# A 2:4-pruned matrix product on one core: six packed tiles and nine pruning pieces in place of seven and six

## The chip, the cores and the metric

The kernel runs on one core of one Trainium2 chip. The metric is device time of one execution in microseconds, lower is better. The time before is the median of seven runs, 235.54 us (235.22 to 235.74).

The engines that matter are TensorE (PE, matrix products and transposes), VectorE (DVE, elementwise), ScalarE (ACT, elementwise copies and absolute values, and an issuer of DMAs) and SyncE (SP, an issuer of DMAs). Each runs its own instructions in order and waits on semaphores for the others.

## The reference

`x` is 16 x 512 x 1024, `w` is 1024 x 1024, `b` has 1024 elements, all bf16. Within each group of four consecutive rows of `w`, and for each column, the entries whose magnitude is at least the second largest of the four are kept, the others become zero. Then x times the pruned w, plus b:

```python
    wg = w.reshape(G, M, D)                       # M = 4, N = 2
    mag = jnp.abs(wg)
    order = jnp.argsort(mag, 1)
    thr = jnp.take_along_axis(mag, order[:, M - N:M - N + 1, :], 1)
    mask = (lambda x, dt: x.astype(dt))(mag >= thr, w.dtype)
    wp = (wg * mask).reshape(D, D)
    return jnp.einsum("bsd,df->bsf", x, wp) + b
```

## The kernel before

The 8192 rows of x are 64 tiles of 128 rows. A tile needs x transposed (the contraction over 1024 runs along partitions, in 8 steps) and the pruned weights in two halves of 512 columns, `FH`.

**Two ways for a tile.** While the weights are being pruned, they lie in a packed layout: partition q holds the four rows of group q, for each of two halves g of the groups (`w_sb`, `wp`; 512 of the 1024 rows each). The first `NPK` = 7 tiles are multiplied straight from that layout, by columns as soon as these are pruned ("packed tiles"). Their x is loaded plainly by `load_x` (line 97), transposed on PE (`transpose`, line 188, tokens `T6a`: tile 6, half g = 0) and copied from PSUM by ACT (`copy_xt`, line 197, tokens `C6a`). The product of tile t with pruning piece i is `mm_piece` (line 208, tokens `M6.1`): four matmuls, one for each row of the group, of as many columns as the piece has. Meanwhile `save` (line 179) writes the pruned weights to a scratch tensor in DRAM and `reload` (line 182) reads them back in natural order into `wp_nat`, one half of the columns at a time. The other 57 tiles ("natural tiles") take x by transposing DMA (`load_batch`, line 239), in batches of 5, 4 and then 8 tiles with three buffers, and 16 matmuls of 512 columns each. Batch 0 is done one column half at a time (line 370), all others a tile at a time (line 380). DVE adds the bias on the way from PSUM (`evac`, line 362).

**Pruning.** `Piece` (line 140) prunes a block of columns of one g in eight steps: absolute value (`abs`), pairwise maximum and minimum (`hi`, `lo`), minimum and maximum of these (`t1`, `t2`), the threshold (`thr`), the comparison (`mask`) and the product (`mult`). Six pieces stand in line 123: four of 256 columns, then two of 512. For the first two, `abs` runs on DVE (line 161), for the others on ACT (line 154). Piece 0 does `mask` and `mult` in two parts, x and y, of two rows of the group each.

**What sets the order.** Lines 251 to 267 write out the order of each engine's work by hand, as lists of tokens; `run` (line 331) emits them as dependences allow, and `seq` (line 61) pins each engine to it. Tokens `F5` are fillers: products of zeros (line 129) that keep PE occupied. Ahead of the list stand 6 fillers of 512 columns and 8 of 128 (lines 341 and 342). After the list: four saves on SP, the first transposed batch, the two reloads, two more batches, and `finish` (line 231) for the packed tiles: their first column half was set aside by ACT (`stage`, line 226, tokens `S5`), the second is still in PSUM; DVE adds the bias to both and ACT issues the store. Two saves (tokens `W5`, `W4`) are issued by ACT.

**Queues.** Loads are issued in the order of lines 104 to 120, all by SP except x tile 6's first half, which ACT issues ahead of its table load (line 106). Every DMA takes one of eight semaphores in turn, and is not issued before the one eight places ahead of it, from either queue, has landed. PSUM has six buffers for products (`psum_o`), one tile's half in each, and two for transposes.

Of the kernel before, what the change touches and what calls it, by code (L numbers as in the profile page):

```python
# [10 lines left out]
def kernel(  # L11
# [8 lines left out]
    P = 128  # L20
    bf16 = mybir.dt.bfloat16
    fp32 = mybir.dt.float32
# [5 lines left out]
    Dout = w.shape[1]  # L28
# [3 lines left out]
    NT = NTOK // P  # L32
    FH = 512
# [3 lines left out]
    xf = x.flatten_outer_dims()  # L37
    of = out.flatten_outer_dims()

    NPK = 7  # L40
    batches = []
    t0 = NPK
    while t0 < NT:
        nb = min((5, 4)[len(batches)] if len(batches) < 2 else 8, NT - t0)
        batches.append((t0, nb))
        t0 += nb

    const = ctx.enter_context(tc.tile_pool(name="const", bufs=1))
    dram = ctx.enter_context(tc.tile_pool(name="dram", bufs=1, space=bass.MemoryType.DRAM))
# [44 lines left out]
    def load_w(g, c0, c1, eng="sp"):  # L94
        issue(eng, w_sb[:, g, :, c0:c1], wv[:, g, :, c0:c1])

    def load_x(ta, tb, g, eng="sp"):
        xs = const.tile([P, tb - ta, HK], bf16, name=f"x_{ta}_{g}")
        issue(eng, xs[:], xv[:, ta:tb, g * HK:(g + 1) * HK])
        for t in range(ta, tb):  # L100
            x_sb[(t, g)] = xs[:, t - ta, :]


    load_w(0, 0, 256)
    load_x(6, 7, 0, "act")
    act(nc.scalar.activation(spark[:, :1], zeros[:, :1], Act.Abs))
    load_x(4, 6, 0)
    load_x(2, 4, 0)
    load_w(0, 256, 512)
    load_x(6, 7, 1)  # L110
    load_x(1, 2, 0)
    load_w(1, 256, 512)
    load_x(2, 4, 1)
    load_w(1, 0, 256)
    load_x(4, 6, 1)
    load_w(0, 512, 1024)
    load_x(0, 2, 1)
    load_x(0, 1, 0)
    load_w(1, 512, 1024)
    sp(nc.sync.dma_start(bias_sb[:], b.partition_broadcast(P)))  # L120


    pieces = [(0, 0, 256), (0, 256, 512), (1, 0, 256), (1, 256, 512), (0, 512, 1024), (1, 512, 1024)]

    ident = const.tile([P, P], bf16)
    make_identity(nc, ident[:])
# [52 lines left out]
    def save(g, c0, c1, eng="sp"):  # L179
        issue(eng, scr_pk[:, g, :, c0:c1], wp[:, g, :, c0:c1])  # L180

    def reload(h):
        fs = slice(h * FH, (h + 1) * FH)
        sp(nc.sync.dma_start(wp_nat[:, :, fs], scr_nat[:, :, fs]))
# [52 lines left out]
    xnat = {}  # L237

    def load_batch(bi):
        if bi >= len(batches):  # L240
            return
        tb, nb = batches[bi]
        xb = xtb.tile([P, KT, 8 * P], bf16, name="xb")
        sp(nc.sync.dma_start_transpose(out=xb[:, :, :nb * P], in_=xf[tb * P:(tb + nb) * P, :]))
        for j in range(nb):
            xnat[tb + j] = xb[:, :, j * P:(j + 1) * P]
# [3 lines left out]

    order = {
        "pe": (
            "T6a F5 T5a T4a F6 T3a T2a F7 M5.0y M4.0y M6.0y M2.0y M5.0x M3.0x T6b T1a M6.0x M3.0y "
            "M4.0x M2.0x M1.0y M1.0x T3b T2b M6.1 M4.1 M3.1 T4b M1.1 M5.1 T5b M2.1 M6.3 M3.3 M4.3 "
            "T1b T0b M5.3 M2.3 M1.3 M3.2 M6.2 M5.2 T0a M4.2 M2.2 M1.2 M0.0y M0.1 M0.2 M0.3 M0.0x "
            "M2.4 M3.4 M1.4 M0.4 M5.4 M4.4 M5.5 M2.5 M1.5 M4.5 M6.4 M0.5 M6.5 M3.5"
        ),
        "dve": (
            "abs0 hi0 lo0 t10 t20 thr0 mask0y mask0x mult0y abs1 mult0x hi1 lo1 t11 t21 thr1 mask1 "
            "mult1 lo3 hi3 t23 t13 thr3 mask3 mult3 lo2 hi2 t22 t12 thr2 mask2 mult2 lo4 hi4 t24 "  # L260
            "t14 thr4 mask4 mult4 hi5 lo5 t25 t15 thr5 mask5 mult5"
        ),
        "act": (
            "C6a C5a C4a C2a C3a C6b C1a abs3 C3b abs2 C2b C4b C5b abs4 C1b abs5 C0a S5 C0b S1 S4 "
            "S6 S2 S0 S3 W5 W4"
        ),
    }
    written = set()
# [4 lines left out]
    def all_of(tok, i):  # L273
        return [tok + x for x in halves.get(i, ("",))]
# [3 lines left out]
        return (tok[:-1] if k else tok), k  # L278

    transposed = []  # L280

    def needs(eng, tok):
        base, k = split_tok(tok)
        if tok[0] == "C":
            return ["T" + tok[1:]]
        if tok[0] == "T":
            return ["C" + transposed[-2]] if len(transposed) > 1 else []
        if tok[0] == "F":
            return []
        if base[0] == "M":  # L290
            t, i = base[1:].split(".")
            key = (int(t), pieces[int(i)][1] // FH)
            slot = []
            if key not in opened and len(opened) >= 6:
                pt, ph = opened[len(opened) - 6]
                slot = [f"S{pt}"] if ph == 0 else []
            return [f"C{t}{'ab'[pieces[int(i)][0]]}", f"mult{i}{k}"] + slot
        if tok[0] == "S":
            return [f"M{tok[1:]}.{n}" for i, pc in enumerate(pieces) if pc[1] < FH for n in all_of(str(i), i)]
        if tok[0] == "W":  # L300
            return all_of("mult" + tok[1:], int(tok[1:]))
        i, step = base[-1], base[:-1]
        before = {"abs": [], "hi": ["abs"], "lo": ["abs"], "t1": ["hi"], "t2": ["lo"],
                  "thr": ["t1", "t2"], "mask": ["thr", "hi", "lo"], "mult": ["mask"]}[step]
        return [b_ + i + (k if b_ == "mask" else "") for b_ in before]

    def emit(eng, tok):
        base, k = split_tok(tok)
        if tok[0] == "T":
            transpose(int(tok[1]), "ab".index(tok[2]))  # L310
            transposed.append(tok[1:])
        elif tok[0] == "F":
            filler(int(tok[1:]))
        elif tok[0] == "C":
            copy_xt(int(tok[1]), "ab".index(tok[2]))
        elif tok[0] == "M":
            mm_piece(*map(int, base[1:].split(".")), part[k])
        elif tok[0] == "S":
            stage(int(tok[1:]))
        elif tok[0] == "W":  # L320
            save(*pieces[int(tok[1:])], eng="act")
        else:
            i = int(base[-1])
            if i not in p:
                p[i] = Piece(i)
            if eng == "act":
                p[i].abs_act()
            else:
                p[i].do(base[:-1], part[k])
# [17 lines left out]
    save(1, 256, 512)  # L347
    load_batch(0)
    reload(0)
    reload(1)  # L350
    load_batch(1)
    load_batch(2)
    for t in (2, 0, 3, 1, 6, 5, 4):
        finish(t)


    def nat_group(xt, ps, c0, c1):
        for kt in range(KT):
            pe(nc.tensor.matmul(ps, lhsT=xt[:, kt, :], rhs=wp_nat[:, kt, c0:c1],  # L359
                                start=(kt == 0), stop=(kt == KT - 1)))  # L360

    def evac(o, ps, c0, c1):
        dve(nc.vector.tensor_tensor(o[:, c0:c1], ps, bias_sb[:, c0:c1], op=Alu.add))  # L363

    def store(eng, t, o, c0=0, c1=Dout):
        issue(eng, of[t * P:(t + 1) * P, c0:c1], o[:, c0:c1])

    for bi, (tb, nb) in enumerate(batches):
        load_batch(bi + 3)
        if bi == 0:  # L370
            outs = [outp.tile([P, Dout], bf16, name="o") for _ in range(nb)]
            for h in range(2):
                for j in range(nb):
                    ps = psum_o.tile([P, FH], fp32, name="ps")
                    nat_group(xnat[tb + j], ps[:], h * FH, (h + 1) * FH)
                    evac(outs[j], ps[:], h * FH, (h + 1) * FH)
                    if h == 1:
                        store("act", tb + j, outs[j])
            continue
        for j in range(nb):  # L380
            t = tb + j
            xt = xnat[t]
            o = outp.tile([P, Dout], bf16, name="o")
            if t == NT - 1:
                for n, (c0, c1) in enumerate(((0, FH), (FH, FH + CW), (FH + CW, Dout - P), (Dout - P, Dout))):
                    ps = psum_o.tile([P, FH], fp32, name="ps")
                    nat_group(xt, ps[:, :c1 - c0], c0, c1)
                    evac(o, ps[:, :c1 - c0], c0, c1)
                    store("act" if n % 2 else "sp", t, o, c0, c1)
            else:  # L390
                pss = [psum_o.tile([P, FH], fp32, name="ps") for _ in range(2)]
                for kt in range(KT):
                    for h in range(2):
                        pe(nc.tensor.matmul(pss[h][:], lhsT=xt[:, kt, :],  # L394
                                            rhs=wp_nat[:, kt, h * FH:(h + 1) * FH],
                                            start=(kt == 0), stop=(kt == KT - 1)))
                for h in range(2):
                    evac(o, pss[h][:], h * FH, (h + 1) * FH)
                    if t >= NT - 6:
                        store("act", t, o, h * FH, (h + 1) * FH)  # L400
                if t < NT - 6:
                    store("act", t, o)
# [30 lines left out]
```

## Time and profile before

| what | us |
|---|---|
| median of seven runs | 235.54 |
| the profiled execution's own time | 235.31 |
| its span, first to last instruction | 233.5 |
| PE busy, natural products of whole tiles (line 394) | 176.3 |
| PE busy, packed products (line 219) | 25.5 |
| PE busy, products done by column half, batch 0 and the last tile (line 359) | 21.1 |
| PE busy, fillers (line 131) | 5.5 |
| PE busy, transposes (line 194) | 5.3 |
| DVE busy in all | 104.3 |
| ACT busy in all | 15.4 |

The span runs from the first to the last instruction of the program; the time of the run also has what lies around it. PE's busy time is modelled at the ends of its matmuls, and what overlaps counts once, so the sums are to be read as shares. The slices of the page (40 of 5.8 us each) show where the engines work: DVE and ACT are dense in the first five slices, the pruning phase, and DVE is at a third or so afterwards.

```profile
PE   8999999999999999999999999999999999999995
DVE  3999559632343343244244234334334424423434
ACT  3678000000000000000000000000000000000000
PEclk9999999999999999999999999999999999999999
DMA  6999979999999972992229921698221221222122
```

### The profile page before, as it was taken

The numbers are of one execution on the slowest core, as the hardware profiler recorded it, in microseconds if no ns is written. First come the engines' busy times: TensorE is split into PE (matmuls) and PEld (weight loads), VectorE is DVE, ScalarE is ACT, GpSimd is POOL, SyncE is SP. The second block draws the span as 40 slices with busy tenths as digits, with TensorE's granted clock in tenths as the row PEclk, the third lists the DMA queues.
The fourth block names the chain that finished last, engine by engine and source line by source line (L and its number), as shares of the span: only waits on it lengthen the run. The fifth ranks groups of instructions, "written<-read, shape, count | busy, mean of one in ns | idle before, by whom it ended". The sixth has DMA issues, their size and how long they took to land.

```text
span 233.5 us, 2871 instructions
## 1 busy us (share of the span) xinstructions
PE 229.9 (98%) x1184; PEld 113.5 (49%) x1184; DVE 104.3 (45%) x177; ACT 15.4 (7%) x27; POOL 0.7 (0%) x6
## 2 busy tenths in 40 slices
PE   8999999999999999999999999999999999999995
PEld 5997444444444444444444444444444444444443
DVE  3999559632343343244244234334334424423434
ACT  3678000000000000000000000000000000000000
POOL 1000000000000000000000000000000000000000
PEclk9999999999999999999999999999999999999999
DMA  6999979999999972992229921698221221222122
GB/s 191 317 300 219 308 224 227 282 261 250 237 322 291 290 156 90 222 271 94 90 80 226 278 83 54 140 225 221 90 90 46 90 93 58 76 90 91 46 90 90
DMA packets 79500, 40.29 MB, mean 173 GB/s; under 512 B 60416, under 2 KB 71936, under 8 KB 79488
## 3 DMA queue, kind: packets, MB, share of 16 engines
q1 hardware_dynamic: 68208, 22.32, 44.5%
q10 hardware_dynamic: 11280, 17.80, 22.6%
q8 instruction: 9, 0.15, 0.3%
q14 instruction: 3, 0.02, 0.0%
HBM read 6.29 MB, written 18.87 MB: 108 GB/s over the span
## 4 chain that ended last, share of the span: by engine, by line
PE 98%; DVE 0%; issue 0%
PE ps L394 75%; PE ps L219 10%; PE ps L359 9%; PE ps L131 2%; PE tp L194 2%; DVE o L363 0%; DVE zeros L80 0%
## 5 line engine op out<-in xcount | busy, mean ns | idle before, releaser
L394 PE MATMUL ps<-wp_nat,xb 128*128 128x512 bf16 x816 | 176.3, 379 | 0.0
L394 PEld LDWEIGHTS <-xb 128*128 128x128 bf16 x816 | 79.9, 98 | 96.3
L363 DVE TENSOR_TENSOR o<-ps,bias_sb 128x512 bf16<-128x512 f32 (+1 forms) x116 | 74.0, 677 | 117.1 <-PE ps L394 110.8
L219 PE MATMUL ps<-wp,xt 128*128 128x256 bf16 (+1 forms) x168 | 25.5, 308 | 0.0
L359 PE MATMUL ps<-wp_nat,xb 128*128 128x512 bf16 (+2 forms) x112 | 21.1, 349 | 0.0
L219 PEld LDWEIGHTS <-xt 128*128 128x128 bf16 x168 | 16.2, 98 | 7.5
L359 PEld LDWEIGHTS <-xb 128*128 128x128 bf16 x112 | 10.3, 98 | 10.7
L233 DVE TENSOR_TENSOR o<-ps,bias_sb 128x512 bf16<-128x512 f32 x7 | 4.8, 687 | 4.9 <-PE ps L219 4.9
L131 PE MATMUL ps<-zeros 128*128 128x128 bf16 (+1 forms) x32 | 5.5, 341 | 1.0 <-DVE zeros L80 1.0
L154 ACT ACTIVATE mag<-w_sb 128x1024 bf16<-128x1024 bf16 (+1 forms) x4 | 6.0, 1489 | 0.3 <-DMA w_sb<-in_w_dram 0.3
L151 DVE TENSOR_TENSOR wp<-w_sb,mag 128x1024 bf16<-128x1024 bf16 (+2 forms) x7 | 5.4, 766 | 0.2
L199 ACT COPY xt<-tp 128x256 f32<-128x256 f32 x14 | 5.0, 374 | 6.2 <-PE tp L194 6.2
L151 DVE TENSOR_TENSOR mag<-mag,hi 128x1024 bf16<-128x1024 bf16 (+2 forms) x7 | 5.3, 767 | 0.2
L194 PE MATMUL tp<-ident,x 128*128 128x128 bf16 x56 | 5.3, 239 | 0.0
L234 DVE TENSOR_TENSOR o<-st,bias_sb 128x512 bf16<-128x512 f32 x7 | 4.8, 682 | 0.0
L194 PEld LDWEIGHTS <-x 128*128 128x128 bf16 x56 | 4.5, 121 | 0.1
L131 PEld LDWEIGHTS <-zeros 128*128 128x128 bf16 x32 | 3.2, 133 | 2.6 <-issue 1.7
L228 ACT COPY st<-ps 128x512 f32<-128x512 f32 x7 | 3.6, 609 | 0.2 <-PE ps L219 0.2
L151 DVE TENSOR_TENSOR hi<-mag 128x512 bf16<-128x512 bf16 (+1 forms) x6 | 3.0, 508 | 0.0
L151 DVE TENSOR_TENSOR lo<-mag 128x512 bf16<-128x512 bf16 (+1 forms) x6 | 3.0, 507 | 0.0
L161 DVE TENSOR_SCALAR mag<-w_sb 128x1024 uint16<-128x1024 uint16 x2 | 0.9, 426 | 3.3 <-DMA w_sb<-in_w_dram 3.3
L151 DVE TENSOR_TENSOR hi<-hi,lo 128x256 bf16<-128x256 bf16 (+1 forms) x6 | 2.0, 337 | 0.2
(11 smaller groups left out, 6.5 us busy)
## 6 DMA issues: line engine op xcount, KB each, us to landing
out_dram<-o ACTq DMA_DIRECT2D x58, 256.0 KB, 4.2
wp_nat<-wp_scratch SPq DMA_DIRECT2D x2, 1024.0 KB, 6.4
x<-in_x_dram SPq DMA_DIRECT2D x5, 256.0 KB, 4.8
out_dram<-o ACTq DMA_DIRECT2D x10, 128.0 KB, 1.7
w_sb<-in_w_dram SPq DMA_DIRECT2D x4, 256.0 KB, 4.7
w_sb<-in_w_dram SPq DMA_DIRECT2D x2, 512.0 KB, 6.7
wp_scratch<-wp SPq DMA_DIRECT2D x4, 256.0 KB, 5.5
wp_scratch<-wp ACTq DMA_DIRECT2D x2, 512.0 KB, 5.3
```

Source lines behind the costliest of these rows:

```text
L131: pe(nc.tensor.matmul(warm_ps[:, :rep * P], lhsT=zeros[:], rhs=zeros[:, None, :].to_broadcast([P, rep, P]), start=True, stop=True))
L151: dve(nc.vector.tensor_tensor(out, a, b_, op=op))
L154: act(nc.scalar.activation(self.mag[:], self.w, Act.Abs))
L194: pe(nc.tensor.transpose(tp[:, m, :], xg[:, m, :], ident[:]))
L199: act(nc.scalar.copy(xt[:].bitcast(fp32), xpk[(t, g)][:].bitcast(fp32)))
L219: pe(nc.tensor.matmul(ps[:, c0 - h * FH:c1 - h * FH], lhsT=xpk[(t, g)][m], rhs=wp[:, g, m, c0:c1], start=(new and m == ms.start), stop=(le ...
L228: act(nc.scalar.copy(st[:], ps_open.pop((t, 0))[:]))
L233: dve(nc.vector.tensor_tensor(o[:, FH:], ps_open.pop((t, 1))[:], bias_sb[:, FH:], op=Alu.add))
L234: dve(nc.vector.tensor_tensor(o[:, :FH], staged.pop(t)[:], bias_sb[:, :FH], op=Alu.add))
L359: pe(nc.tensor.matmul(ps, lhsT=xt[:, kt, :], rhs=wp_nat[:, kt, c0:c1], start=(kt == 0), stop=(kt == KT - 1)))
L363: dve(nc.vector.tensor_tensor(o[:, c0:c1], ps, bias_sb[:, c0:c1], op=Alu.add))
L394: pe(nc.tensor.matmul(pss[h][:], lhsT=xt[:, kt, :], rhs=wp_nat[:, kt, h * FH:(h + 1) * FH], start=(kt == 0), stop=(kt == KT - 1)))
```

## The change

- Six packed tiles in place of seven; tile 6 becomes a natural tile, so there are 58 of them.
- Nine pruning pieces in place of six: (g, first column, end) = two of 128 columns, then seven of 256. DVE's list interleaves neighbouring pieces, so that an operation of one stands between two dependent ones of another. DVE takes the absolute values of pieces 0, 1 and 2, ACT those of pieces 3 to 8.
- The first weight load is split into two of 128 columns. x tile 5 takes the place of tile 6 as the one that ACT loads first, and ACT also issues the load of tiles 2 and 3 (half g = 0), still ahead of its table load. The other loads are rearranged on SP, and one of them falls away.
- New written orders for PE, DVE and ACT. Fillers in PE's list: 12 and 8 in place of 5, 6 and 7.
- The saves of columns 512 to 1023 are still one for each g (`wsave`), each after both of its pieces: `W6` and `W8`.
- Batches of natural tiles: 3, 3, 4, then 8. The first two batches (`LEAD` = 2) are done together by column half: all six tiles' first halves, then all second halves with their stores. On SP, the second batch's transposed load stands between the two reloads.

```diff
-    NPK = 7
+    NPK = 6
     batches = []
     t0 = NPK
-    while t0 < NT:
-        nb = min((5, 4)[len(batches)] if len(batches) < 2 else 8, NT - t0)
+    for nb in (3, 3, 4, 8, 8, 8, 8, 8, 8):
         batches.append((t0, nb))
         t0 += nb
+    LEAD = 2
...
-    load_w(0, 0, 256)
-    load_x(6, 7, 0, "act")
+    load_w(0, 0, 128)
+    load_x(5, 6, 0, "act")
+    load_w(0, 128, 256)
+    load_x(2, 4, 0, "act")
     act(nc.scalar.activation(spark[:, :1], zeros[:, :1], Act.Abs))
-    load_x(4, 6, 0)
-    load_x(2, 4, 0)
     load_w(0, 256, 512)
-    load_x(6, 7, 1)
-    load_x(1, 2, 0)
+    load_x(4, 5, 0)
+    load_x(0, 2, 0)
+    load_w(1, 0, 256)
+    load_x(2, 4, 1)
     load_w(1, 256, 512)
-    load_x(2, 4, 1)
-    load_w(1, 0, 256)
     load_x(4, 6, 1)
     load_w(0, 512, 1024)
     load_x(0, 2, 1)
-    load_x(0, 1, 0)
     load_w(1, 512, 1024)
...
-    pieces = [(0, 0, 256), (0, 256, 512), (1, 0, 256), (1, 256, 512), (0, 512, 1024), (1, 512, 1024)]
+    pieces = [(0, 0, 128), (0, 128, 256), (0, 256, 512), (1, 0, 256), (1, 256, 512), (0, 512, 768), (0, 768, 1024), (1, 512, 768), (1, 768, 1024)]
...
         "pe": (
-            "T6a F5 T5a T4a F6 T3a T2a F7 M5.0y M4.0y M6.0y M2.0y M5.0x M3.0x T6b T1a M6.0x M3.0y "
...
-            "M2.4 M3.4 M1.4 M0.4 M5.4 M4.4 M5.5 M2.5 M1.5 M4.5 M6.4 M0.5 M6.5 M3.5"
+            "T5a F12 T3a T2a F8 M5.0y M3.0y M5.1 M2.1 M2.0y T4a M3.1 M5.0x M2.0x T1a T0a M3.0x "
...
+            "M2.5 M1.5 M3.5 M4.5 M5.5 M1.6 M2.6 M0.6 M5.6 M4.6 M3.6 M2.7 M3.7 M5.7 M0.7 M4.7 M1.7 "
+            "M4.8 M1.8 M3.8 M0.8 M5.8 M2.8"
         ),
         "dve": (
-            "abs0 hi0 lo0 t10 t20 thr0 mask0y mask0x mult0y abs1 mult0x hi1 lo1 t11 t21 thr1 mask1 "
...
+            "abs0 lo0 hi0 t20 abs1 t10 hi1 lo1 t11 t21 thr0 thr1 mask0y mask1 mult0y mult1 abs2 "
+            "mask0x lo2 mult0x hi2 t22 t12 thr2 mask2 mult2 hi3 lo3 t13 t23 thr3 mask3 lo4 mult3 "
...
+            "mask6 lo7 mult6 hi7 t27 t17 thr7 mask7 hi8 mult7 lo8 t28 t18 thr8 mask8 mult8"
         ),
         "act": (
-            "C6a C5a C4a C2a C3a C6b C1a abs3 C3b abs2 C2b C4b C5b abs4 C1b abs5 C0a S5 C0b S1 S4 "
-            "S6 S2 S0 S3 W5 W4"
+            "C5a C3a C2a C4a C1a C0a abs3 C3b C2b abs4 C4b C5b abs5 C1b C0b abs6 S5 S2 S3 abs7 S4 "
+            "S1 S0 abs8 W6 W8"
         ),
...
+    wsave = {6: (0, 512, 1024), 8: (1, 512, 1024)}
...
     load_batch(0)
     reload(0)
+    load_batch(1)
     reload(1)
-    load_batch(1)
     load_batch(2)
-    for t in (2, 0, 3, 1, 6, 5, 4):
+    for t in (3, 2, 1, 0, 4, 5):
         finish(t)
...
+    lead = [t for tb, nb in batches[:LEAD] for t in range(tb, tb + nb)]
+    outs = {t: outp.tile([P, Dout], bf16, name="o") for t in lead}
+    for h in range(2):
+        for t in lead:
+            ps = psum_o.tile([P, FH], fp32, name="ps")
+            nat_group(xnat[t], ps[:], h * FH, (h + 1) * FH)
+            evac(outs[t], ps[:], h * FH, (h + 1) * FH)
+            if h == 1:
+                store("act", t, outs[t])
+                for bi in range(LEAD):
+                    if t == batches[bi][0] + batches[bi][1] - 1:
+                        load_batch(bi + 3)
+
     for bi, (tb, nb) in enumerate(batches):
+        if bi < LEAD:
+            continue
         load_batch(bi + 3)
...
```

## The prediction

> **What bounds the kernel now.** I read the page's first and fourth parts, then the waits of the matmul engine, then the chain of waits in order of time, then VectorE's timeline.
>
> ```profile
> PE 229.9 (98%) x1184; PEld 113.5 (49%) x1184; DVE 104.3 (45%) x177; ACT 15.4 (7%) x27; POOL 0.7 (0%) x6
> PE 98%; DVE 0%; issue 0%
> ```
>
> ```profile
> PE ps L131 <- DVE zeros L80: 1.0, 1, 1.0
> ```
>
> TensorE (PE) waits once, 1.0 us at the very start, and never again. So a wait removed elsewhere is worth nothing: the time is PE's start, plus what PE is given to do, plus 2.6 us of tail, which the change leaves as it is. The chain shows how much that is (start us, us, what):
>
> ```profile
> 6.81 0.45 PE tp L194 x8
> 7.26 0.39 PE ps L131 x7
> 7.65 1.31 PE ps L219 x12
> 18.84 15.14 PE ps L219 x84
> 33.98 17.27 PE ps L359 x80
> 51.25 176.12 PE ps L394 x816
> ```
>
> These are my prices, all at full clock and including the weight load that goes with each matmul: a transpose 0.45/8 = 0.056 us, a filler 0.39/7 = 0.056, a 256-column product 1.31/12 = 0.109, a 512-column product 17.27/80 = 0.216. A natural tile (16 products of 512) costs 3.454. The first packed product starts at 7.65, the packed phase ends at 33.98.
>
> VectorE (DVE) prunes the weights. Its timeline (start us, us):
>
> ```profile
> 3.94 0.43 DVE L161 TENSOR_SCALAR mag<-w_sb 128x1024 uint16<-128x1024 uint16 x1 [3.01 <-DMA w_sb<-in_w_dram]
> 4.40 0.43 DVE L151 TENSOR_TENSOR hi<-mag 128x512 bf16<-128x512 bf16 x1
> 4.74 0.42 DVE L151 TENSOR_TENSOR lo<-mag 128x512 bf16<-128x512 bf16 x1
> 5.08 0.28 DVE L151 TENSOR_TENSOR hi<-hi 128x256 bf16<-128x256 bf16 x1
> 5.28 0.28 DVE L151 TENSOR_TENSOR lo<-lo 128x256 bf16<-128x256 bf16 x1
> 5.60 0.29 DVE L151 TENSOR_TENSOR hi<-hi,lo 128x256 bf16<-128x256 bf16 x1
> 10.88 0.42 DVE L151 TENSOR_TENSOR lo<-mag 128x512 bf16<-128x512 bf16 x1
> 13.73 0.42 DVE L151 TENSOR_TENSOR lo<-mag 128x512 bf16<-128x512 bf16 x1
> 25.27 1.23 DVE L151 TENSOR_TENSOR wp<-w_sb,mag 128x2048 bf16<-128x2048 bf16 x1
> ```
>
> The first load lands at 3.94, the last product of pruning ends at 25.27 + 1.23 = 26.50. By the written order PE then still has 28 products of piece 5 and 4 of piece 4, 32 × 0.216 = 6.9, which would end at 33.4; the packed phase ends at 33.98, so DVE has about 0.6 us of room. Read start to start, 512 elements a partition cost 0.34 (4.40 to 4.74) and 256 cost 0.20 (5.08 to 5.28); 1024 cost 0.60 by the same view. An instruction that needs the one just before it costs 0.12 more (5.28 to 5.60).
>
> **The change, part 1: PE's ledger.** Transposes fall from 56 to 48, written-out fillers rise from 18 to 20. Ahead of the first product stood 20 transposes and 18 fillers, now 12 and 20: −8 + 2 = −6 × 0.056 = −0.33, so it can start at 7.32. After it, 36 transposes stand in both kernels. Packed products were 7 × 16 = 112 of 256 columns and 7 × 8 = 56 of 512: 12.24 + 12.09 = 24.33. They become 6 × 8 = 48 of 128 columns and 6 × 28 = 168 of 256. The trace has no 128-column product. The nearest row, eight transposes with their own weights, gives 0.056; the other bound is the 256-column price, 0.109. I take 0.056, which is the same shape of matmul (the upper end would add 48 × 0.053 = 2.5): 2.69 + 18.36 = 21.05, that is −3.28. The tile that is no longer packed becomes natural: +3.454. Sum: −0.33 − 3.28 + 3.45 = **−0.16 us** if PE still never waits, and the packed phase would end at 33.98 − 0.33 − 3.28 = 30.37.
>
> The Trainium skill, "TensorE: Matmul & The Clock Gate", section "Back-to-back issue gap", speaks against such narrow products: it gives about 81 ns for each of a stream of 128-column matmuls with their weight loads. By it the 48 would cost 1.2 us more (an estimate from that page) and the sum would be 236.7, slower. This trace's eight transposes in 0.45 us disagree, and the measurement decides.
>
> **Part 2: DVE's ledger.** One tile fewer means 3.6 us less cover, and the same weights now go through nine pieces instead of six. A 128-wide piece has operations half as wide as rows above: 0.13 for 128 elements by the step from 0.34 to 0.20, and about 0.20 for its absolute value. Pieces 0 and 1 together: 3.46 plus one dependence 0.13 (interleaving hides the others). Piece 2 up to its product: 0.34 × 3 + 0.20 × 3 + 0.60 + 3 × 0.125 = 2.60. Then to the start of piece 8's product six pieces at 2.73 to 2.85: the upper value is 10.88 to 13.73, the lower one has the wait between mask and product filled by the next piece's first operation. That is 16.4 to 17.1, middle 16.7. With the last product, 0.69 by its 1024-element form, pruning ends 3.6 + 2.6 + 16.7 + 0.7 = 23.6 us after its first load lands (bounds 23.3 to 23.95); before it was 22.56. PE then still owes piece 8's products, 24 × 0.109 = 2.62, and 0.05 to hand over. So by DVE the packed phase ends at landing + 26.3 (26.0 to 26.6), against PE's own 30.37: **the two meet where the landing is about 4.0.** DVE goes from 0.6 us of room to none; past that point each 0.1 us is paid in full.
>
> **Part 3: when that load lands.** The DMA engines are full in those microseconds (columns: stretch, its length, busy time by engine with counts, PE clock, DMA share, GB/s):
>
> ```profile
> 2.60:3.40 0.80, 0.80 (x3) 0.30 (x2) 0.00 (x0) 0.06 (x1) 0.00 (x0) 1.00 1.02 284
> 50.00:54.00 4.00, 4.00 (x20) 1.86 (x19) 0.94 (x2) 0.00 (x0) 0.00 (x0) 1.00 1.28 290
> ```
>
> So I count bytes at 284 GB/s. Before, 262 KB of weights and 131 KB of x had landed at 3.94. Now the first load is 131 KB: 0.46 earlier, 3.46, if nothing else intrudes. But ACT's queue now sends 262 KB of x tiles 2-3 right behind tile 5, 0.92 us of the same engines: 4.4 if all of it gets in between. Middle 3.92. Piece 1's weights come behind all of it, 655 KB in all: 4.84, and DVE asks for them 0.86 after its start, so the effective start is max(3.92, 3.98), about 4.0 (3.5 to 4.4 so far).
>
> These weights come in packets of 256 bytes, where 512 were used. In the lower row the queue moved only packets under 512 B, those of the transposed x loads, at 290 GB/s, no slower per byte. The other bound is that such a packet costs what a 512-byte one costs in the upper row: then the two loads count as 524 KB, 0.92 more, and the effective start is 4.9. I take the lower row, it being the same size of packet on the same queue. DVE's end is then 30.3, PE's 30.37; over the bounds the excess is 0 to 0.8. Since each group of products waits for its own piece, and not only the last, I take 0.1.
>
> The Trainium skill, "DMA: Bandwidth & Descriptors", section "Specifications", asks for 512 B and more for line rate and names a read-modify-write below. If that read-modify-write doubled the packets' time (an estimate from that page), the sum would be 236.2; the 290 GB/s speak against it for transposed loads, and for weights no row does.
>
> **Part 4: moves that cost nothing, and their cover.** ACT's table load (1.28 us from 1.16) slides behind one more DMA issue, 0.4 to 0.6: ready at about 3.1; its first copy ran at 5.04, after PE's first transposes. Without that cover the 0.6 would reach the first product. On SP's queue the later loads move up by one issue, about 0.6. The second transposed load now stands ahead of the second reload there: its issue, 6.05 us for five tiles by the timeline and so 3.6 for three, is over before the saves that the reload waits for have landed. Saves of columns 512 and up are issued by ACT after its last absolute value, one after piece 6 and one after piece 8 (27.6, against 27.14 for the later one before). Late transfers:
>
> ```profile
> wp_nat<-wp_scratch SPq DMA_DIRECT2D x1, 1024.0 KB, 6.8
> xb<-in_x_dram SPq DMA_TRANSPOSE x1, 16.6
> ```
>
> The second reload was issued at 32.9 and landed at 39.7, the four-tile transposed load behind it at 49.9; needed at 42.6 and 51.25. Now: save at 27.6, landed by 33.3, reload at 40.1, four tiles at 50.5. Two leading batches of three tiles run their first half in 6 × 8 × 0.216 = 10.4 us, so the reload is needed at 30.4 + 10.4 = 40.8 and the four tiles at 51.1. Both fit by 0.6. Cost 0, bounds 0 to 1.5.
>
> **Sum.** −0.16 + 0.1 = −0.06. On the profiled execution: span 233.5 and 1.8 around it, 235.31, gives 235.25. That execution lies 0.23 under the median of the runs, 235.54, so the median should be **235.48**. The measurement of this kernel can't tell less than 0.2% (0.47 us) from no change.
>
> **Rivals.** *Faster:* DVE is never late and the whole ledger counts: 235.38; even so within 0.2%. Below 235.07 another 0.3 us would have to come from outside the ledger; against it stands that PE has no wait to lose. *Slower, the pruning starts late:* x tiles 2-3 and narrow packets hold the first weights; it decides from an effective start of 4.1 and is over 0.2% from 4.7, since −0.16 + (4.7 + 26.3 − 30.37) = 0.47. At the upper bound, 4.9, it gives +0.67: 236.2. For it: full engines. Against it: the lower DMA row. *Slower, a late transfer:* the leading tiles' stores now begin at about 43 while the four transposed tiles arrive (before, no store was issued from 40.2 to 49.95). Three more stores of 262 KB are 2.8 us of engine time; if two thirds of it delays the load beyond 51.1, +1.3: 236.7. For it: 16.6 us for four tiles, which stores stretch already. Against it: three of the six stores of packed tiles now go out ahead of the reload. *The change doesn't do what it says:* x tiles 2-3 land no earlier than the 6.6 at which PE took them before; PE reaches them now at 5.01 + 12 fillers at the cold price of F5 (0.53/5), 6.3, and stalls 0.3: 235.8.
>
> **How the numbers follow.** Forecast with its faster variant, within 0.2%: 0.64; the last rival, also within: 0.05. Late pruning past the bound 0.15, late transfer 0.11: slower 0.26. Faster past the bound 0.05. Range: from 235.15 (full ledger and its noise) to 236.4 (late pruning at its upper bound, and a little of the late transfer); the likeliest case alone is 235.3 to 235.9.
>
> **What will show it.** First product near 7.3; the waits of PE free of DVE beyond some tenths in sum; the last pruning product ending near 27.6; packed phase ending near 30.4; the natural products without a wait. Wrong if PE waits over 0.7 us in sum, for DVE in the packed phase or for a DMA at the leading tiles, or if 128-column products step by more than 0.056.

## The result and the profile after

The change made the kernel slower: 239.9 us median of 12 runs (236.87 to 243.31), against 235.54 before (31 runs). The ratio is 1.0136, 95% interval [1.0114, 1.0158]; it is made without the runs that lie more than 1.5% above the fastest of their kernel, which is why it is less than the ratio of the two medians. The prediction was 235.48, within 0.2%, with a range up to 236.4.

The spread is new too: 6.4 us, where the kernel before has 1.8 in the same comparison. The execution that was profiled is one of the longer ones, 242.27 us with a span of 240.5.

The page's slices and its chain that ended last:

```profile
PE   8899998499999999999999999999999999999995
PEclk9999999689999999999999999999999999999999
PE 80%; DVE 9%; DMA 9%; issue 1%; SPq 0%
```

Before, the chain was 98% PE. Now 9% of it is DMA and 9% DVE, PE has a hole in the eighth slice (42 to 48 us), and in the same slices the granted clock falls. The waits of PE, besides the 1.0 at its start:

```profile
PE ps L364 <- DMA wp_nat<-wp_scratch: 3.8, 1, 3.8
PE ps L219 <- DVE wp L151: 0.6, 1, 0.6
```

The 0.6 is at the first packed product, one of the places that the prediction said to watch. The 3.8 is the second reload, which it had costed at nothing. The chain in order of time (start us, us, what):

```profile
27.34 0.70 DVE wp L151
28.07 7.76 DMA wp_scratch<-wp
35.89 9.22 DMA wp_nat<-wp_scratch
45.16 13.03 PE ps L364 x48
58.19 176.12 PE ps L404 x816
```

Pruning ends, the later save takes 7.76 us to land, the reload that waits for it 9.22, and only then do the leading tiles' second halves start. These 48 products take 13.03 us, where 48 × 0.216 = 10.4. The reason stands in the busy time by stretch (stretch, its length, PE, PEld, DVE, ACT and POOL busy with counts, granted clock, DMA share, GB/s):

```profile
41.40:43.40 2.00, 0.00 (x0) 0.00 (x0) 0.69 (x1) 0.00 (x0) 0.00 (x0) 1.00 1.11 354
43.40:45.10 1.70, 0.00 (x0) 0.00 (x0) 0.00 (x0) 0.00 (x0) 0.00 (x0) 0.51 1.01 135
45.20:50.20 5.00, 5.00 (x12) 1.75 (x13) 0.69 (x1) 0.00 (x0) 0.00 (x0) 0.50 0.84 179
50.40:58.00 7.60, 7.60 (x37) 3.43 (x35) 2.77 (x4) 0.00 (x0) 0.00 (x0) 1.00 0.70 178
```

PE's clock is halved 2.0 us after it falls idle, and stays so until about 50.2, 5 us into its work.

For this execution the whole difference is now accounted for on the chain. The natural tiles that are done whole start at 58.19 in place of 51.25, 6.94 later; the spans differ by 7.0. By part: the first natural product starts at 30.87 in PE's timeline, which is 31.04 on the chain (the two views lie 0.17 apart at this place, as 30.74 and 30.91 do in the kernel with held stores below). So the packed phase is 2.94 shorter, the one natural tile more takes 3.45, together **+0.5**; the reload makes PE wait **3.8**; the halved clock costs 13.03 − 10.36 = **2.7**. Everything after it is unchanged (176.12 us in both chains). The other executions were not profiled; how long each of them waited is not shown.

### The profile page after: what moved, and what is told of

Read it like the earlier page. It is cut to its first block, busy times and chain, and to the rows that moved or that the text cites. A ratio compares the mean times of both kernels' runs of the same rounds, so it can differ in the third digit from the quotient of the medians.

```text
span 240.5 us, 3011 instructions
## 1 busy us (share of the span) xinstructions
PE 232.4 (97%) x1242; PEld 117.7 (49%) x1242; DVE 105.8 (44%) x199; ACT 14.2 (6%) x26; POOL 0.7 (0%) x6
## 4 chain that ended last, share of the span: by engine, by line
PE 80%; DVE 9%; DMA 9%; issue 1%; SPq 0%
PE ps L404 73%; PE ps L364 7%; DMA wp_nat<-wp_scratch 4%; DMA wp_scratch<-wp 3%; DVE hi L151 3%; DVE wp L151 2%; DVE mag L151 2%; DVE lo L151 2%; DMA w_sb<-in_w_dram 2%; SPq L93 0%; DVE mag L161 0%; DVE o L368 0%; SPq L184 0%
## 5 line engine op out<-in xcount | busy, mean ns | idle before, releaser
L368 DVE TENSOR_TENSOR o<-ps,bias_sb 128x512 bf16<-128x512 f32 (+1 forms) x118 | 75.4, 678 | 125.6 <-PE ps L404 110.8
L404 PEld LDWEIGHTS <-xb 128*128 128x128 bf16 x816 | 79.9, 98 | 96.3
L364 PE MATMUL ps<-wp_nat,xb 128*128 128x512 bf16 (+2 forms) x128 | 27.2, 376 | 3.8 <-DMA wp_nat<-wp_scratch 3.8
L219 PE MATMUL ps<-wp,xt 128*128 128x256 bf16 (+1 forms) x216 | 22.2, 261 | 0.6 <-DVE wp L151 0.6
L364 PEld LDWEIGHTS <-xb 128*128 128x128 bf16 x128 | 12.5, 103 | 18.3 <-DMA wp_nat<-wp_scratch 4.3
L219 PEld LDWEIGHTS <-xt 128*128 128x128 bf16 x216 | 19.2, 98 | 2.7 <-issue 0.7
L154 ACT ACTIVATE mag<-w_sb 128x1024 bf16<-128x1024 bf16 x6 | 6.5, 1078 | 0.0
L199 ACT COPY xt<-tp 128x256 f32<-128x256 f32 x12 | 4.0, 376 | 6.6 <-PE tp L194 6.6
L194 PE MATMUL tp<-ident,x 128*128 128x128 bf16 x48 | 4.1, 227 | 0.0
L194 PEld LDWEIGHTS <-x 128*128 128x128 bf16 x48 | 3.4, 116 | 0.0
L161 DVE TENSOR_SCALAR mag<-w_sb 128x512 uint16<-128x512 uint16 (+1 forms) x3 | 1.0, 336 | 3.6 <-DMA w_sb<-in_w_dram 3.6
```

The lines of the kernel that those rows point to most:

```text
L154: act(nc.scalar.activation(self.mag[:], self.w, Act.Abs))
L194: pe(nc.tensor.transpose(tp[:, m, :], xg[:, m, :], ident[:]))
L199: act(nc.scalar.copy(xt[:].bitcast(fp32), xpk[(t, g)][:].bitcast(fp32)))
L219: pe(nc.tensor.matmul(ps[:, c0 - h * FH:c1 - h * FH], lhsT=xpk[(t, g)][m], rhs=wp[:, g, m, c0:c1], start=(new and m == ms.start), stop=(le ...
L404: pe(nc.tensor.matmul(pss[h][:], lhsT=xt[:, kt, :], rhs=wp_nat[:, kt, h * FH:(h + 1) * FH], start=(kt == 0), stop=(kt == KT - 1)))
```

## The experiments

Two transfers had been put beside the late saves and the second reload: the second batch's transposed load (written ahead of the reload on SP) and, since the packed phase is 3 us shorter, the packed tiles' stores (from 31.1 in place of mostly after 33.6). The rival was that six packed tiles simply give too little cover, that is, too little work for PE while the weights that are pruned last go to DRAM and back. All results are against the kernel before, on the same chip.

**One batch of six leading tiles, no load between the reloads.**

```diff
-    for nb in (3, 3, 4, 8, 8, 8, 8, 8, 8):
+    for nb in (6, 4, 8, 8, 8, 8, 8, 8):
-    LEAD = 2
+    LEAD = 1
...
-    load_batch(1)
     reload(1)
+    load_batch(1)
```

> The six leading natural tiles are loaded as one batch ahead of the first reload, and no transposed load stands between the two reloads any more. Theory 'transposed load in the way' (it shares the DMA engines with the two late saves, and the second reload waits for these): the later save lands by 33.5 in place of 35.8, the second reload by 40.5 in place of 45.1, PE waits under 0.5 us for it, its clock stays at 1.00; the longer first load (about 7 us of issue) may cost 0.3 to 0.6 at the first reload, 236.0 to 236.6 us. Rival 'too little cover' (six packed tiles and later pruning are enough by themselves): the second reload still lands after 43 and the time stays above 238.

Measured: 238.16 us median (237.28 to 241.21), ratio 1.009 [1.0052, 1.0127]. The later save landed at 33.6 and the second reload at 40.6, both within 0.1 of what the first theory had, and PE waited for neither. But the six-tile load held up the first reload, which landed at 32.2:

```profile
PE ps L364 <- DMA wp_nat<-wp_scratch: 1.5, 1, 1.5
```

This wait stands at 30.8 to 32.35, before the first halves. The cover is too short for that arrangement, by 1.5 us and not by the 0.3 to 0.6 expected, and so the time missed the expected 236.0 to 236.6. The late wait went with the load. In this profile PE's clock stayed at 1.00 through the wait of 1.5; three of the ten runs have a mean clock of 0.993.

**The kernel before with the load between.**

```diff
-    reload(1)
     load_batch(1)
+    reload(1)
```

> The kernel before with one line moved: the second batch's transposed load (four tiles) ahead of the second reload, nothing else of the change. Theory 'transposed load in the way': the two saves by ACT take 7 to 11 us to land in place of 5.0 to 5.7, the second reload lands at 43 to 46 in place of 39.7, PE, which needs it at 42.6, waits 0.5 to 3.5 us: 236 to 241 us. Rival 'too little cover': as before, 235.5, since seven packed tiles and the old pruning are all there.

Measured: 243.89 us (242.95 to 246.28), ratio 1.0321 [1.0247, 1.0395], worse than expected. PE's wait, and the time from issue to landing of the two saves and of the transposed load that was moved, in its profile (KB each, median us to landing):

```profile
PE ps L359 <- DMA wp_nat<-wp_scratch: 8.3, 1, 8.3
```

```profile
wp_scratch<-wp ACTq DMA_DIRECT2D x2, 512.0 KB, 16.0
xb<-in_x_dram SPq DMA_TRANSPOSE x1, 18.3
```

One line moved, with seven packed tiles and the old pruning in place, makes the saves land after 16 us in place of 5.0 to 5.7. The reload then lands at 51.6, where 43 to 46 was expected, and PE waits 8.3. So the place of a transposed load ahead of the second reload costs by itself, and cover is not what is missing there.

**Fillers in the wait.**

```diff
+        if h == 1:
+            keep = psum_t.tile([P, 4, P], bf16, name="tp")
+            kf = keep[:].bitcast(fp32).rearrange("p a b -> p (a b)")
+            for _ in range(40):
+                pe(nc.tensor.matmul(kf, lhsT=zeros[:], rhs=zeros[:, None, :].to_broadcast([P, 2, P]),
+                                    start=True, stop=True))
```

> The changed kernel with 40 fillers of 256 columns (40 x 0.109 = 4.4 us) on PE between the leading tiles' first and second halves, where PE waited 3.8 us in the profile; the transfers are left as they are. Theory 'part of the loss is the clock' (in the profile the granted clock was 0.50 from 43.4 to 50.3, after the idle stretch): the clock stays at 1.00, the second reload lands at 45 as before, and the time is that of the changed kernel's runs without a drop of the clock, 237 to 240, with less spread, no run above 240.5. Rival 'the clock costs nothing': no change, 237 to 243.

Measured: 240.25 us, four runs from 240.01 to 240.41, ratio 1.0149 [1.0099, 1.0199]. The reload landed at 43.6, late again, though 1.5 earlier than in the changed kernel's profile. The granted clock stayed at 1.00 in all four runs:

```profile
41.40:45.80 4.40, 4.40 (x42) 3.90 (x40) 0.69 (x1) 0.00 (x0) 0.00 (x0) 1.00 1.15 156
45.80:50.00 4.20, 4.15 (x21) 1.95 (x21) 1.20 (x2) 0.00 (x0) 0.00 (x0) 1.00 0.91 229
```

The fillers end at 45.83, behind both landings of the reload, 43.6 here and 45.12 in the changed kernel's profile. So the 240.4 us of this profile can be set against the 242.3 of that one; the spread shrinks from 6.4 us in twelve runs to 0.4 in four. The time is the fillers' 4.36 us (41.47 to 45.83) on top of the 235.9 that the next kernel reaches without a wait. The median is no better than the changed kernel's 239.9, since the fillers take their 4.36 us in every run, however long it would have waited. So idling costs twice: the wait, and the clock after it. The changed kernel's spread agrees: its runs at full clock throughout lie at 236.9 to 239.5, those with a mean clock of 0.993 at 239.7 to 241.2, with 0.986 at 242.3 and 243.3. The kernels below whose profile has no wait for the reload kept 0.999 or more in every run.

**The packed tiles' stores held back.**

```diff
-        issue("act", of[t * P:(t + 1) * P, :], o[:])
+        held.append((t, o))
...
                 store("act", t, outs[t])
+                while held:
+                    store("act", *held.pop(0))
```

(with 12 output buffers in place of 10)

> The changed kernel with the six packed tiles' stores held back on ACT until the first leading tile's second half is stored (and 12 output buffers for them in place of 10). Theory 'the stores slow the second reload' (its 1 MB landed 9.2 us after issue, 6.8 before, while 0.9 MB of stores passed): the later save still lands at 35 to 36, the reload takes 6.5 to 7.2 and lands by 43, PE waits 1.5 to 2 us in place of 3.8, 236.5 to 239. Theory 'transposed load in the way' alone: the reload is as late as in the changed kernel, 44.5 to 45.5, and the time unchanged.

Measured: 235.88 us median (235.28 to 237.78), ratio 0.9996 [0.9967, 1.0026]. The loss is gone, more fully than expected. PE has no wait but the one at the start; the reload:

```profile
PE ps L131 <- DVE zeros L81: 1.0, 1, 1.0
```

```profile
wp_nat<-wp_scratch SPq DMA_DIRECT2D x1, 1024.0 KB, 5.6
```

It takes 5.6 us in place of 9.2 and lands at 39.9; PE comes for it at 41.1. The later save landed at 34.3, still late against the 33.3 that was forecast: the transposed load is still there.

**The buffers alone.**

```diff
-    outp = ctx.enter_context(tc.tile_pool(name="outp", bufs=10))
+    outp = ctx.enter_context(tc.tile_pool(name="outp", bufs=12))
```

> The changed kernel with 12 output buffers in place of 10 and nothing else: the part of the run with held stores that might have helped by itself. Theory 'the stores slow the second reload': as the changed kernel, the reload issued at 34.5 to 36 and 8.5 to 9.5 us long, PE waiting 2 to 4 us for it, 237 to 243 us. Rival 'the output buffers were the bound': 235.5 to 236.5 and no wait.

Measured: 238.37 us (236.8 to 240.93), ratio 1.0101 [1.0071, 1.0131]; in its profile

```profile
PE ps L364 <- DMA wp_nat<-wp_scratch: 3.6, 1, 3.6
```

with the reload issued at 34.9 and 9.8 us long. The buffers do not take the loss away; it was the stores.

**The second load's traffic left out.** The second batch's three tiles are multiplied with the first batch's x, so this kernel leaves out their own products; PE's work is the same.

```diff
         tb, nb = batches[bi]
+        if bi == 1:
+            for j in range(nb):
+                xnat[tb + j] = xnat[batches[0][0] + j]
+            return
```

> The changed kernel without the second batch's transposed load; its three tiles are multiplied with the first batch's x, so that the matmuls are as many as before and 0.75 MB of traffic between the two reloads is left out. The stores stay where they are. Theory 'transposed load in the way': the two saves land in 5 to 6.5 us in place of 10.9 and 7.8, the second reload is issued at 33 to 33.7 in place of 35.9 and, with the stores still beside it, takes 7 to 9 us: landed by 40.5 to 42.5, PE waits 0 to 1.5 us, 235.5 to 237.5. Rival 'stores alone': the later save at 34.3 to 35.8 as it was, the reload at 43 to 45, 237 to 243.

Measured: 235.96 us (235.67 to 236.8), ratio 1.0017 [1.0001, 1.0033], and no wait for the reload. The later save and the reload:

```profile
wp_scratch<-wp ACTq DMA_DIRECT2D x1, 512.0 KB, 3.5
```

```profile
wp_nat<-wp_scratch SPq DMA_DIRECT2D x1, 1024.0 KB, 7.1
```

The save lands 3.5 us after its issue, at 31.5, in place of 35.8. And the reload, though the stores are where they were, lands at 38.6: it was issued at 31.6, when only one of the stores (31.3) stood ahead of it, and the others, from 32.6 on, landed after 43.5. So in the changed kernel either of the two alone is bearable: the stores without the load here, the load without the stores in the kernel with held stores. Together they are not: with the load the save lands 3 to 4 us later (34.3 to 35.8 in place of 31.5), in this time three stores become ready and go ahead of the reload, and with the stores it takes 3.7 us longer (9.2 in place of 5.6).

**Held stores, and x tiles 2-3 behind the narrow weight loads.** This undoes the part of the change that ACT's queue took on.

```diff
-    load_x(2, 4, 0, "act")
     act(nc.scalar.activation(spark[:, :1], zeros[:, :1], Act.Abs))
+    load_x(2, 4, 0)
     load_w(0, 256, 512)
```

> The kernel with held stores, and x tiles 2-3 (first half) loaded by SP behind the two narrow weight loads in place of by ACT between them. Theory 'x tiles 2-3 hold up piece 1's weights' (landed at 5.2 to 5.5 where DVE could have started on them at 4.9): these land by 4.9, the first packed product starts at 7.0 to 7.3 without a wait, the packed phase ends 0.2 to 0.5 earlier, near 30.4; the time 235.2 to 235.6, within 0.3% of the kernel before. Rival 'narrow packets are what is slow': piece 1's weights still land after 5.2 and the first product waits 0.3 us or more.

The landing of piece 1's weights in the changed kernel, issued at 1.49 (beside x tiles 2-3 on ACT), and in this one, issued at the same time:

```profile
x<-in_x_dram ACTq DMA_DIRECT2D x1, 256.0 KB, 3.8
w_sb<-in_w_dram SPq DMA_DIRECT2D x1, 128.0 KB, 4.0
```

```profile
w_sb<-in_w_dram SPq DMA_DIRECT2D x1, 128.0 KB, 3.0
```

They land at 4.47 in place of 5.47, the first product starts at 7.24 without a wait, the packed phase ends 0.24 us before that of the kernel with held stores (first natural product at 30.50, against 30.74). So the place of x tiles 2-3 is what held these weights up, and not the narrow packets. The 0.24 is as much as was expected, but it is not shown to come from the weights: in neither of the two profiles does PE wait for them. The half clock at the start lasted longer in the kernel with held stores, where the eight transposes ahead of the last fillers take 0.85 us and here 0.67, and by that alone the first product comes 0.19 later there. In the time nothing shows: 236.01 us (235.45 to 237.18), ratio 1.0029 [1.0011, 1.0047], where 235.2 to 235.6 was expected.

**Only the first three stores held.**

```diff
-        held.append((t, o))
+        if t in (3, 2, 1):
+            held.append((t, o))
+        else:
+            issue("act", of[t * P:(t + 1) * P, :], o[:])
```

> As the kernel with held stores and x tiles 2-3 behind, but only the first three packed tiles' stores (ready at 31 to 34, before the second reload can be issued) are held; the other three go out when they are ready, at 35 to 37. Theory 'stores ready before the reload is issued stand ahead of it': the reload still lands by 41.2 (5.5 to 6.5 us after its issue at 34.9), the later three stores land behind it, at 42 to 45, and PE does not wait: 235.3 to 236.2, no worse than all six held. Rival 'any store beside the reload slows it by its bytes': the reload takes 7.5 us or more, lands at 42.4 or later, PE waits over 1 us, 237 or more.

Measured: 238.6 us (236.91 to 240.69), ratio 1.0125 [1.0078, 1.0171], where 235.3 to 236.2 was expected. In the profile, that of one of the shorter runs (237.22), the reload took 6.6 us, between the two forecasts, and landed at 42.55; PE waited 0.5 for it, after another loss earlier:

```profile
PE tp L194 <- DMA x<-in_x_dram: 1.5, 2, 0.8
PE ps L368 <- DMA wp_nat<-wp_scratch: 0.5, 1, 0.5
```

One of the three later stores was ready at 35.5, before the reload's issue at 35.9, and went ahead. With no store held the reload took 9.0 to 9.8 (three profiles), with the first three held 6.6, with all six 5.5 to 5.6 (three profiles): most of the delay belongs to the three that are issued first. The remaining 1 us may be the one store ahead of it or the two beside it; the run doesn't part these theories. Where the longer runs lost their time is not shown; two of them have a mean clock of 0.993. With all six held, the next kernel took 235.94 on the same chip.

**One held store after each leading tile.**

```diff
-                while held:
+                if held:
```

> As the kernel with held stores and x tiles 2-3 behind, but the six held stores go out one after each leading tile's own store and not all after the first. Theory 'twelve stores at once squeeze the first eight-tile load' (landed at 64.3, needed at 65.0): that load lands by 63 and the slower runs of that kernel (up to 237.2) go: median 235.3 to 235.7, highest under 236.5. Rival: same bytes by the same time, no difference, median 235.7 to 236.1.

Measured: 235.94 us (235.06 to 236.58), ratio 1.0011 [0.9995, 1.0026]. The first eight-tile load landed at 64.6, as late as with all stores at once. The highest run is lower, the median is not: a miss. No version ran faster than the kernel before.

## Why the prediction was wrong, point by point

**PE's ledger** held in its prices. A 128-column product, which no row had shown, costs 0.056: in the kernel with held stores, whose chain is PE throughout, 26 of them take 1.45 us.

```profile
7.15 0.45 PE ps L131 x8
7.59 1.00 PE ps L219 x14
9.78 1.45 PE ps L219 x26
30.91 0.22 PE ps L365
```

Its sum was 0.5 us off: the first product starts at 7.59 there (forecast 7.32), since the half clock of the start lasted longer, and the packed phase ends at 30.91 (forecast 30.37). The forecast counted the six instructions fewer at full clock, but they stand where the clock may still be half: twelve fillers ahead of the first product take 1.28 us there, 0.107 each, and the eight behind them 0.056. In all profiles with the new pruning and x tiles 2-3 on ACT's queue the first product starts at 7.3 to 7.7, against 7.65 before; in four of the six PE had to wait for DVE there. So the −0.33 of this term came out anywhere between its size and nothing. Nothing would be gained or lost with an end at 33.98 − 3.45 = 30.53; 30.91 is 0.38 later, which is this kernel's whole difference in the profiles, 235.69 against 235.31.

**DVE's ledger** was right. From the first load's landing to the end of pruning it took 4.06 to 28.03 = 24.0, of which 0.5 was a wait for piece 1's weights; the forecast was 23.6 without it.

```profile
4.06 0.29 DVE L161 TENSOR_SCALAR mag<-w_sb 128x512 uint16<-128x512 uint16 x1 [3.12 <-DMA w_sb<-in_w_dram]
5.50 0.29 DVE L161 TENSOR_SCALAR mag<-w_sb 128x512 uint16<-128x512 uint16 x1 [0.48 <-DMA w_sb<-in_w_dram]
27.34 0.69 DVE L151 TENSOR_TENSOR wp<-w_sb,mag 128x1024 bf16<-128x1024 bf16 x1
```

Piece 1's weights landed at 5.47, forecast 4.84. With the 0.86 of the forecast that is an effective start of 4.6, inside its bounds of 3.5 to 4.9. The seventh experiment shows that x tiles 2-3 on ACT's queue were the cause: piece 1's weights landed at 5.1 to 5.5 in six profiles with that load there, at 4.5 to 4.9 in the three without. This rival, late pruning, came true at a small size: by its own sum, −0.16 + (4.6 + 26.3 − 30.37) = 0.4 us, it would have left the result within 0.2%.

**Part 4 is the step that failed.** "Now: save at 27.6, landed by 33.3, reload at 40.1 ... Both fit by 0.6. Cost 0, bounds 0 to 1.5." The save was issued at 28.07 and landed at 35.83, the reload at 45.12. Both durations had been taken over from before, 5.7 and 6.8, although the same part noted that a transposed load now stood ahead of the reload: it asked when the load's issue would be over, and not what its packets do to the saves beside it. Even the issue took 8.9 us (22.07 to 30.98) and not 3.6. With the load in flight the save took 7.8 us (3.5 without it), and with the stores the reload took 9.2 (5.6 without them). By the prediction's own sign, PE waiting over 0.7 us in sum for DVE or for a DMA, it was wrong: 0.6 and 3.8.

**The late-transfer rival** had the right kind of mechanism at the wrong place, and its argument against was upside down: "three of the six stores of packed tiles now go out ahead of the reload" was counted as relief for the transposed load behind it. It is the reload, and with it PE, that these three delay: holding them alone took it from 9.2 to 6.6 us. The four-tile load itself landed at 49.1, before the 51.1 at which the forecast needed it.

**A term was missing.** The sum had no price for PE idling. A wait was costed one to one; here 3.8 us cost another 2.7. This price is not a constant. In the profile of the buffers alone a wait of 3.6 cost another 1.5, since the 48 products behind it took 44.73 to 56.55 = 11.82 in place of 10.36:

```profile
44.73 1.46 PE ps L364 x3
46.41 10.14 PE ps L364 x44
56.55 1.08 PE ps L404 x5
```

The mean clock of that run is 0.992. And the wait of 1.5 in the first experiment's profile left the clock at 1.00. The Trainium skill, "TensorE: Matmul & The Clock Gate", section "What's actually happening", gives half clock after an idle window of about 3.4 us, judged in windows that run on their own. The drop here lasts from 43.4 to 50.2, which is the length of two such windows, but it came 2.0 us after PE's last product, before a whole window had been idle; the measurement decides. The missing term alone does not explain the miss: for a wait of 1.5, the upper bound of part 4, it is nothing by that profile, and the bound itself was too low, since it was built on undisturbed transfers.

**ACT's table load** behind one more issue cost nothing, as forecast: its first copy ran at 5.05 (5.04 before). The expected order of PE's trouble was wrong: not the pruning that feeds the packed phase, but the trip of its results through DRAM.

## What to carry to other kernels

A transfer's duration in a profile holds for the neighbours that it had there. When a change starts other transfers earlier, list for each late transfer which ones will be in flight or ready before it can be issued, and price it with them. The latency row of before is no bound in either direction: the reload took 6.8 there, 5.6 with the stores held, 9.2 in the changed kernel. A sum of bytes comes near here, as an estimate made afterwards: four of the six stores landed ahead of the reload, 4 × 262 KB at the 284 GB/s of the prediction's row are 3.7 us, and 5.6 + 3.7 = 9.3. And where the busiest engine would wait a few microseconds, add what its clock may lose afterwards, here 1.5 and 2.7 us for waits of 3.6 and 3.8.

## What the runs showed of the hardware

- A transposed load beside plain copies on another queue: the later 0.5 MB save took 3.5 us without one in flight, 6.3 to 7.8 with one of three tiles; the two saves took 5.0 and 5.7 in the kernel before and 16 there with one of four tiles.
- The order of issue mattered: the stores issued from 31.1 to 33.6 landed ahead of the 1 MB reload that was issued at 35.9, and so did the one issued right behind it (at 40.5, the reload at 45.1). Stores issued 0.5 us after the reload or later landed behind it, 8 to 11 us after their own issue. The Trainium skill, "Trainium Kernel Development and Optimization", section "Key Constraints", says that the queues of SP and ACT run on the same 16 DMA engines. These runs agree: ACT's save is slowed by SP's load, and SP's reload by ACT's stores.
- PE waits of 3.6 and 3.8 us lowered its granted clock to a half in the profiles, 2.0 us after the last product in the longer one; a wait of 1.5 in another profile did not. The same stretch filled with products of zeros kept it at 1.00.
